# A new written-out order for the middle pairs, and five unread products behind the experts, in a fused attention, soft-mixture and gated kernel

## The chip, the cores and the metric

The kernel runs on one core of one Trainium2 chip. The time is device microseconds (us) of one execution. Engines are called PE (TensorE; PEld are its weight loads), DVE (VectorE), ACT (ScalarE), POOL (GpSimd) and SP (the queue that issues most DMAs). PEclk is the clock granted to PE, as a share of full speed.

## What is computed

```python
def reference(q, k, v, phi, w1, w2, w_gate, w_val, w_out, rms_g):   # cut to the formulas
    q_pool = q.reshape(4, 8, 576, 2, 64).mean(axis=3)       # q, k, v: 4 batches, 8 heads, 1152 x 64
    s = q_pool @ k.T / 8
    p = exp(s - s.max(-1));  a = (p / p.sum(-1)) @ v         # 576 x 64 a head
    x = a, heads side by side                               # 2304 tokens x 512
    logits = x @ phi                                        # 32 slots
    d = softmax of logits over all tokens;  slots = d.T @ x
    slot_out[e] = relu(slots[e] @ w1[e]) @ w2[e]            # 8 experts, 4 slots each
    x = softmax of logits over the slots @ slot_out
    xn = x / sqrt(mean(x * x) + 1e-6) * rms_g
    return (silu(xn @ w_gate) * (xn @ w_val)) @ w_out       # 1536 wide, result 2304 x 512
```

## The kernel before

**Stages.** Sixteen *pairs* of heads (p = 0 to 15) go through the attention one after the other, then come the eight experts, a short stage that multiplies small matrices out of the slots' outputs (lines 1110 to 1126), and the gated stage, whose product with w_out fills the end.

**The order of a pair is written out by hand.** Every engine takes its instructions in program order. For each pair a string of step names (FIRST for pair 0, PLAN for pairs 1 to 13, LAST_2 for pair 14, LAST for pair 15; lines 34 to 62) gives that order, and the loop at lines 853 to 871 calls one function a name. The steps that matter here, in pair p:

- `m` (wide_item, lines 311 to 335): a product of PE for the row maxima of pair p+1 into two PSUM banks, and a reduction of DVE over it. There are nine in a pair; the last three stand together behind `q81`.
- `q` and two digits (qk, line 374): eight products of PE into two PSUM banks: three parts of the scores, and a product (operands mr and pick) that subtracts the row maxima. Then an exponential on ACT (line 385). Eighteen in a pair.
- `e` and two digits (add_e, line 390): adds these tiles up on POOL (line 401; two operands in SBUF), for the sums of the rows. Fourteen of the eighteen issue an addition.
- `v` and a digit (av, line 403): 16 matmul records of PE, exponentials by values.
- `rest_k` (line 286) and `sum_q` (line 248): a DMA that adds into SBUF, issued on POOL's queue.
- `load_64`, `abs_64`, `turn_64`, `spill` (lines 639 to 704, 631): the three large matrices of the gated stage arrive as 64-bit numbers. `load_64` fetches 512 KB, `abs_64` makes two passes of ACT over it, `turn_64` one pass of DVE with two operands in SBUF (line 698), and `spill` writes the result to DRAM. There are up to three of each in a pair, 36 turned tiles in all.
- `load_ew` (line 776): a piece of the experts' weights.
- `sums`, `inverse`, `recips`, `x_turn`, `x_divide`, `x_logits`, `logit_add` (lines 418 to 502): what is left of pair p-1: its row sums, their inverses, the division and the logits.
- `high_q`, `low_q`, `round_k`, `less_k`, `block_q`, `max_red`, `max_row`, `send_row`, `ta`, `tb`: the operands of pairs p+1 and p+2, in two parts each, and the row of negated maxima, which four small DMAs of SP bring into the tile mr. `low_q` is a DVE pass with two operands in SBUF too (line 268).

**Buffers.** The two-bank PSUM tiles rotate through four buffers (line 176), so a product waits until the one four tiles earlier is read. SBUF tiles come from sets of equal slots (A, B, C, W). While pairs run, the tile of `v` (from `v0` to the next pair's `take_x`) holds one of the four PSUM buffers.

**hold** (line 198) issues products of constant tiles into a PSUM bank that nobody reads. Before the change it is used at lines 910, 926, 957 and 962, between the attention and the experts.

```python
PLAN = """
m take_x load_q q00 load_k sum_q q01 q10 m q11 q20 q21 e00 e10 e20 e01 m q30 q31 e30 e11 c_exp rest_k q40 m e21 e31
q41 e40 load_ew e41 q50 q51 m turn_64 q60 load_ew q61 e50 e60 q70 m q71 q80 q81 c_soft round_k abs_64 m round_k m m v0
...
```

Of the kernel before, what the change touches and what calls it, by code (L numbers as in the profile page):

```python
# [37 lines left out]
less_k ta v21 v41 v51 send_row v11 v71 v61 v81  # L38
"""
PLAN = """  # L40
m take_x load_q q00 load_k sum_q q01 q10 m q11 q20 q21 e00 e10 e20 e01 m q30 q31 e30 e11 c_exp rest_k q40 m e21 e31
q41 e40 load_ew e41 q50 q51 m turn_64 q60 load_ew q61 e50 e60 q70 m q71 q80 q81 c_soft round_k abs_64 m round_k m m v0
spill e51 v1 e61 sums e70 e80 e71 e81 max_red x_logits inverse inverse max_row load_v d_back v2 less_k v3 c_soft
abs_64 v4 high_q abs_64 v5 c_soft low_q block_q logit_add pair_up recips x_turn d_copy turn_64 slot_part x_divide
x_divide v6 d_turn tb d_exp slot_copy ta drop_x c_turn turn_64 load_64 slot_turn v7 load_64 send_row c_soft v8 load_64
"""
LAST_2 = """
m take_x load_q q00 load_k sum_q q01 load q10 m q11 load q20 load q21 e00 e10 e20 e01 m load q30 q31 e30 e11 c_exp
rest_k load q40 m e21 e31 load q41 e40 load_ew e41 load q50 q51 m turn_64 load q60 load_ew load q61 e50 e60 q70 m q71
load q80 q81 c_soft round_k abs_64 m round_k m m v0 spill e51 v1 e61 sums e70 e80 e71 e81 max_red x_logits inverse  # L50
inverse max_row load_v d_back v2 less_k v3 c_soft abs_64 v4 high_q abs_64 v5 c_soft low_q block_q logit_add pair_up
recips x_turn d_copy turn_64 slot_part x_divide x_divide v6 d_turn tb d_exp slot_copy ta drop_x c_turn turn_64 load_64
slot_turn v7 load_64 send_row c_soft v8 load_64
"""
LAST = """
take_x q00 load_64 sum_up sum_up load_q load_k load q01 e00 e01 c_exp turn_64 load_ew load q10 load q11 spill e10 e11
# [39 lines left out]
def attention_softmoe_gated_kernel(ctx: ExitStack, tc: tile.TileContext, kT, qT, vv, ip, cst, w1, w2, wg, wv, wo, rg, out):  # L96
# [15 lines left out]
    def take(tag, shape, dt, name):  # L112
        assert free[tag] > 0, (tag, name)
        free[tag] -= 1
        return pool.tile(shape, dt, tag=tag, bufs=size[tag], name=name)
# [4 lines left out]
    def B(shape, dt, name):  # L120
        return take("B", shape, dt, name)
# [53 lines left out]
    def two_banks(name):  # L175
        return ps.tile([128, 2, 512], F32, tag="u", bufs=4, name=name)

    def bank(shape, name):
        if not attention[0]:
            return ps.tile(shape, F32, tag="u", bufs=6, name=name)  # L180
        n = 1
        for x in shape[1:]:
            n *= x
        t = two_banks(name)[0:shape[0], 0, 0:n]
        if len(shape) == 3:
            t = t.rearrange("p (a b) -> p a b", a=shape[1])
        elif len(shape) == 4:
            t = t.rearrange("p (a b c) -> p a b c", a=shape[1], b=shape[2])
        return t
# [8 lines left out]
    def hold(o, n):  # L198

        for _ in range(n):  # L200
            pe.matmul(o, lhsT=pick[0], rhs=mr[1][:, 0:512], start=True, stop=True)
# [16 lines left out]
    tb = one.tile([128, 128], F32R, name="tb")  # L218
# [570 lines left out]
    with tc.manual_schedule():  # L789
# [317 lines left out]
        pull()  # L1107


        sos = B([128, 512], F32, "sos")  # L1110
        ac.copy(sos[:, 0:256], so[:, 0:256])
        dv.tensor_copy(sos[:, 256:512], so[:, 256:512])
        o = bank([128, 4, 32], "gto")
        for k in range(4):
            pe.matmul(o[:, k, :], lhsT=sos[:, 128 * k:128 * k + 128], rhs=stack[:, 0:32], start=True, stop=True)
        gT, soT = pt[:, 0], pt[:, 1]
        ac.copy(soT, o)
        dv.tensor_tensor(out=gT, in0=o, in1=rgt[:, :, None].to_broadcast([128, 4, 32]), op=ALU.mult)
        o = bank([128, 32], "gram")
        for k in range(4):  # L1120
            for i in range(4):
                pe.matmul(o[32 * i:32 * i + 32, :], lhsT=soT[:, k, :], rhs=soT[:, k, :], start=(k == 0), stop=(k == 3))
        gram = tb[:, 0:32]
        ac.copy(gram, o)
        dv.tensor_tensor(out=gram[64:128], in0=o[64:128], in1=f(gram[64:128]), op=ALU.subtract)
# [188 lines left out]
```

## Time and profile before

| what | value |
|---|---|
| three runs | 698.14, 704.37, 704.47 us; median 704.37 |
| the profiled execution | 706.88 us, its span 705.0 us |
| mean granted clock of PE | 0.983 |
| busy, share of the span | PE 95%, PEld 69%, POOL 64%, DVE 62%, ACT 57% |
| attention, pairs 0 to 15 | to 446 us |
| experts | about 459 to 498 us |
| gated stage | to the end |

The span runs from the first to the last instruction; 1.9 us of the execution lie around it. A busy share is an average over stages with different limits, so waits are read stage by stage below.

### The profile page before, as it was taken

To read this page: it belongs to the slowest core of one execution; us is meant where nothing else is said; L and a number is where in the kernel's file an instruction comes from. 1 tells how busy PE (TensorE), PEld (TensorE's weight loads), DVE (VectorE), ACT (ScalarE), POOL (GpSimd) and SP (SyncE) were. 2 spreads that over 40 slices of the span, in tenths; PEclk is the share of its full clock that TensorE was granted. 3 is DMA by queue.
4 is the path that set the end of the run, shared out by engine and by line. 5 is a ranking of instruction groups with operands and counts; after the bars stand their busy time and mean duration, and the time that the engine had idled before them with its cause. 6 is when DMAs were issued, how large, how long until landed. Compare 5 with 4: busy or idle time off the path is not lost.

```text
span 705.0 us, 17788 instructions
## 1 busy us (share of the span) xinstructions
PE 672.0 (95%) x7314; PEld 488.6 (69%) x7314; DVE 439.2 (62%) x595; ACT 400.8 (57%) x814; POOL 451.4 (64%) x368
## 2 busy tenths in 40 slices
PE   4999999999999999999999999999899999999998
PEld 3776775775766766757757666644577788888887
DVE  5766777777778788778788676421245755544420
ACT  3674974876768768647867544532146655444420
POOL 6689987978779779678797594000057855534420
PEclk9999999999999999999999999999689999999999
DMA  6345555966867765557466359899950100000000
GB/s 216 102 153 136 136 145 177 278 184 193 222 184 217 213 190 160 141 178 218 134 206 175 125 187 376 268 354 385 385 191 1 45 31 16 30 31 30 31 31 30
DMA packets 58040, 114.66 MB, mean 163 GB/s; under 512 B 6252, under 2 KB 20072, under 8 KB 57960
## 3 DMA queue, kind: packets, MB, share of 16 engines
q1 hardware_dynamic: 53928, 100.86, 41.2%
q0 software_dynamic: 4032, 12.68, 10.7%
q8 instruction: 57, 0.93, 0.5%
q14 instruction: 23, 0.19, 0.1%
HBM read 99.29 MB, written 14.16 MB: 161 GB/s over the span
## 4 chain that ended last, share of the span: by engine, by line
PE 85%; DVE 9%; DMA 2%; ACT 1%; POOL 1%; issue 1%; DVEq 0%; ACTq 0%; POOLq 0%
PE av L408 21%; PE yo L1215 20%; PE sc L383 17%; PE mxp L321 4%; DVE w L698 4%; DVE mx L322 4%; PE gv L1167 3%; PE sums L431 2%; PE hin L980 2%; PE xo L471 1%; PE so L1005 1%; PE part L1146 1%; DMA w<-in_w_dram 1%; PE mxp L331 1%; PE sumt L441 1%; PE xl L489 1%
## 5 line engine op out<-in xcount | busy, mean ns | idle before, releaser
L401 POOL TENSOR_TENSOR acc<-acc,e 128x576 f32<-128x576 f32 x153 | 230.0, 1516 | 10.9 <-ACT e L385 3.4
L385 ACT ACTIVATE e<-sc 128x576 f32<-128x576 f32 x288 | 167.8, 651 | 24.8 <-PE sc L383 19.4
L322 DVE TENSOR_REDUCE mx<-mxp 128x2 f32<-128x1024 f32 x120 | 145.4, 1224 | 57.4 <-PE mxp L321 57.4
L408 PE MATMUL av<-e,vt 128*32 128x288 f32 x2304 | 156.7, 415 | 0.0
L401 POOL TENSOR_TENSOR acc<-e 128x576 f32<-128x576 f32 x63 | 95.0, 1508 | 44.0 <-ACT e L385 44.0
L408 PEld LDWEIGHTS av<-e,vt 128*32 128x32 f32 x2304 | 69.2, 111 | 61.9 <-issue 9.7
L1215 PE MATMUL yo<-woh,hA 128*128 128x512 f32 (+1 forms) x312 | 98.7, 385 | 0.3 <-POOL hA L1198 0.2
L383 PE MATMUL sc<-qh,kh 64*128 64x288 f32 x576 | 87.9, 298 | 0.4 <-DVE mx L303 0.4
L383 PE MATMUL sc<-mr,pick 64*128 64x288 f32 x576 | 86.4, 293 | 0.0
L383 PE MATMUL sc<-qh,kl 64*128 64x288 f32 x576 | 86.4, 293 | 0.0
L383 PE MATMUL sc<-ql,kh 64*128 64x288 f32 x576 | 86.4, 292 | 0.0
L1198 POOL TENSOR_TENSOR hA<-hu,hA 128x384 fp32r<-128x384 f32 x48 | 48.8, 1018 | 43.6 <-ACT hA L1197 43.5
L1172 DVE SCALAR_TENSOR_TENSOR th<-th,gv 128x384 f32<-128x384 f32 x72 | 39.8, 553 | 57.3 <-ACT th L1169 57.1
L1215 PEld LDWEIGHTS yo<-woh,hA 128*128 128x128 f32 x312 | 57.6, 188 | 10.9 <-POOL hA L1198 1.1
L321 PE MATMUL mxp<-kh,qh 64*128 64x512 f32 x240 | 48.5, 420 | 16.6 <-DVE mx L322 16.6
L1169 ACT ACTIVATE th<-gv 128x384 f32<-128x384 f32 x72 | 35.2, 490 | 50.7 <-PE gv L1167 48.4
L383 PEld LDWEIGHTS sc<-qh,kl 64*128 64x128 f32 x576 | 55.6, 186 | 3.6
L383 PEld LDWEIGHTS sc<-qh,kh 64*128 64x128 f32 x576 | 55.3, 186 | 3.9 <-issue 0.9
L1215 PE MATMUL yo<-wol,hA 128*128 128x512 f32 (+1 forms) x151 | 57.8, 383 | 0.0
L383 PEld LDWEIGHTS sc<-mr,pick 64*128 64x128 f32 x576 | 55.7, 186 | 0.0
L383 PEld LDWEIGHTS sc<-ql,kh 64*128 64x128 f32 x576 | 55.5, 185 | 0.0
L698 DVE SCALAR_TENSOR_TENSOR w<-w,raw 128x512 uint32<-128x512 uint32 x36 | 51.9, 1443 | 0.0
(211 smaller groups left out, 1033.9 us busy)
## 6 DMA issues: line engine op xcount, KB each, us to landing
w<-in_w_dram SPq DMA_DIRECT2D x84, 256.0 KB
w<-in_w_dram SPq DMA_DIRECT2D x22, 512.0 KB
vt<-in_vv_dram SPq DMA_DIRECT2D x16, 576.0 KB
away<-w SPq DMA_DIRECT2D x36, 256.0 KB
w<-away SPq DMA_DIRECT2D x36, 256.0 KB
kraw<-in_kT_dram SPq DMA_DIRECT2D x15, 576.0 KB
kl<-in_kT_dram POOLq DMA_DIRECT2D x15, 576.0 KB, 5.8
raw<-in_wg_dram SPq DMA_DIRECT2D x12, 512.0 KB
```

The lines of the kernel that those rows point to most:

```text
L321: pe.matmul(o[:, s, :], lhsT=q[r, 128 * t:128 * t + 128], rhs=k[r, 512 * c:512 * c + 512], start=True, stop=True)
L322: dv.reduce_max(out=heads[:, :, t, c], in_=o, axis=AX.X)
L383: pe.matmul(o[:, s, 0:HQ], lhsT=w[r, wk], rhs=q[r, c], start=(i == 0), stop=(i == 3))
L385: ac.activation(ets[p, kt, h], o[:, :, 0:HQ], AF.Exp, scale=0.0625)
L401: eng.tensor_tensor(out=acc[p, h, j], in0=first[p, h, j] if n == 1 else acc[p, h, j], in1=e, op=ALU.add)
L408: pe.matmul(avt[p][g:g + 32, h, 0:HQ], lhsT=vt[p][:, kt, g:g + 32], rhs=ets[p, kt, h][:, g // 64], start=(n == 1), stop=(n == NKT))
L698: dv.scalar_tensor_tensor(out=y, in0=y, scalar=3, in1=lo, op0=ALU.logical_shift_left, op1=ALU.bitwise_or),
L1167: pe.matmul(o[i], lhsT=sg[n][:, 256 * i + 128 * c:256 * i + 128 * c + 128], rhs=cT[g], start=True, stop=True)
L1169: ac.activation(t, o[0], AF.Tanh, scale=0.5)
L1172: dv.scalar_tensor_tensor(out=t, in0=t, scalar=1.0, in1=o[0], op0=ALU.add, op1=ALU.mult)
L1198: gp.tensor_tensor(out=b, in0=u, in1=f(a), op=ALU.subtract)
L1215: pe.matmul(o, lhsT=x, rhs=w[:, c], start=(ft == 0 and i == 0), stop=(ft == NF - 1 and i == 2))
```

## The change

PLAN and LAST_2 get the same steps in another order; no step is added or taken away, and the `load` steps of LAST_2 keep their number. Behind the experts five unread products are issued, in three places.

```diff
 PLAN = """
-m take_x load_q q00 load_k sum_q q01 q10 m q11 q20 q21 e00 e10 e20 e01 m q30 q31 e30 e11 c_exp rest_k q40 m e21 e31
-q41 e40 load_ew e41 q50 q51 m turn_64 q60 load_ew q61 e50 e60 q70 m q71 q80 q81 c_soft round_k abs_64 m round_k m m v0
-spill e51 v1 e61 sums e70 e80 e71 e81 max_red x_logits inverse inverse max_row load_v d_back v2 less_k v3 c_soft
-abs_64 v4 high_q abs_64 v5 c_soft low_q block_q logit_add pair_up recips x_turn d_copy turn_64 slot_part x_divide
-x_divide v6 d_turn tb d_exp slot_copy ta drop_x c_turn turn_64 load_64 slot_turn v7 load_64 send_row c_soft v8 load_64
+take_x load_q m load_k sum_q q00 q01 q10 m q11 q20 e00 q21 m e01 e10 e20 e11 c_exp q30 e30 q31 rest_k q40 load_ew e21
+c_soft m e31 q41 e40 q50 e41 m e50 q51 q60 q61 q70 turn_64 m load_ew spill e60 q71 q80 q81 round_k round_k m m m e70
+e51 load_v e80 sums v0 v1 abs_64 e61 abs_64 e71 v2 d_back load_64 e81 max_red v3 v4 x_logits less_k inverse d_copy
+inverse high_q block_q c_soft max_row low_q x_turn recips abs_64 logit_add slot_part c_soft pair_up x_divide x_divide
+turn_64 v5 v6 d_turn send_row tb c_turn ta slot_copy turn_64 d_exp drop_x slot_turn c_soft v7 load_64 load_64 v8
 """
...
+        still = bank([128, 512], "hold")
+        hold(still, 2)
         sos = B([128, 512], F32, "sos")
         ac.copy(sos[:, 0:256], so[:, 0:256])
         dv.tensor_copy(sos[:, 256:512], so[:, 256:512])
         o = bank([128, 4, 32], "gto")
         for k in range(4):
             pe.matmul(o[:, k, :], lhsT=sos[:, 128 * k:128 * k + 128], rhs=stack[:, 0:32], start=True, stop=True)
+        hold(still, 1)
         gT, soT = pt[:, 0], pt[:, 1]
         ac.copy(soT, o)
...
                 pe.matmul(o[32 * i:32 * i + 32, :], lhsT=soT[:, k, :], rhs=soT[:, k, :], start=(k == 0), stop=(k == 3))
+        hold(still, 2)
         gram = tb[:, 0:32]
         ac.copy(gram, o)
```

LAST_2 is changed in the same way (its ten `load` steps stand between the score steps as before).

## Rows read from the trace of the kernel before

**Rows 1.** The page's 40 slices of the span: PE's granted clock in tenths.
```profile
PEclk9999999999999999999999999999689999999999
```

**Rows 2.** Waits of PE: waiter, releaser, us in total, times, longest.
```profile
PE mxp L321 <- DVE mx L322: 16.6, 11, 1.6
```

**Rows 3.** Timeline of PE in pairs 3 and 5: start, us, what, [idle before].
```profile
106.16 0.73 PE L321 MATMUL mxp<-kh,qh 64*128 64x512 f32 x4 [1.61 <-DVE mx L322]
...
156.43 0.40 PE L321 MATMUL mxp<-kh,qh 64*128 64x512 f32 x2
...
158.26 0.41 PE L321 MATMUL mxp<-kh,qh 64*128 64x512 f32 x2
...
161.79 0.73 PE L321 MATMUL mxp<-kh,qh 64*128 64x512 f32 x4 [1.55 <-DVE mx L322]
```

**Rows 4.** Timeline of DVE in pair 5.
```profile
156.87 1.23 DVE L322 TENSOR_REDUCE mx<-mxp 128x2 f32<-128x1024 f32 x1 [0.61 <-PE mxp L321]
158.01 2.59 DVE L698 SCALAR_TENSOR_TENSOR w<-w,raw 128x512 uint32<-128x512 uint32 x1
160.52 1.21 DVE L322 TENSOR_REDUCE mx<-mxp 128x2 f32<-128x1024 f32 x1
```

**Rows 5.** Timeline of POOL in pair 5.
```profile
156.34 1.44 POOL L401 TENSOR_TENSOR acc<-e 128x576 f32<-128x576 f32 x1
157.72 0.87 POOL L287 DMA_DIRECT2D kl<-in_kT_dram  x1
158.33 6.29 POOL L401 TENSOR_TENSOR acc<-acc,e 128x576 f32<-128x576 f32 x4
```

**Rows 6.** Line 698 by itself: min, median, max of its duration in ns.
```profile
L698 DVE SCALAR_TENSOR_TENSOR w<-w,raw x36: 669/1056/2656, 87.9 to 418.9; 128x512 uint32<-128x512 uint32 x36
```

**Rows 7.** Timelines of POOL and DVE: a pass in a lone issue, one among additions.
```profile
176.15 0.88 POOL L250 DMA_DIRECT2D qs<-in_qT_dram  x1 [2.18 <-PE pto L568]
...
176.54 0.68 DVE L698 SCALAR_TENSOR_TENSOR w<-w,raw 128x512 uint32<-128x512 uint32 x1
...
226.15 1.05 DVE L698 SCALAR_TENSOR_TENSOR w<-w,raw 128x512 uint32<-128x512 uint32 x1
```

**Rows 8.** Windows by pair (3, 7, 10): us, busy PE, PEld, DVE, ACT, POOL; clock.
```profile
93.51:121.94 28.43, 26.82 (x351) 18.74 (x351) 21.19 (x23) 18.80 (x35) 22.91 (x18) 0.94 0.60 168
...
205.19:231.88 26.69, 25.34 (x351) 18.20 (x351) 21.28 (x24) 20.39 (x43) 22.52 (x16) 1.00 0.75 218
...
288.02:316.88 28.86, 27.31 (x357) 19.42 (x357) 21.61 (x24) 18.78 (x35) 21.89 (x16) 0.94 0.55 164
```

**Rows 9.** Windows behind the experts, columns as in rows 8.
```profile
500.00:502.00 2.00, 1.49 (x44) 1.30 (x48) 0.53 (x3) 0.19 (x1) 0.00 (x0) 0.52 1.08 387
...
516.00:518.00 2.00, 2.00 (x15) 1.49 (x7) 0.77 (x2) 1.59 (x4) 1.50 (x3) 0.71 1.05 386
```

**Rows 10.** Timeline of PE behind the experts.
```profile
498.48 1.09 PE L1115 MATMUL gto<-cs,sos 128*128 128x32 f32 x8 [0.47 <-ACT sos L1111]
499.92 0.57 PE L1122 MATMUL gram<-pt 128*32 128x32 f32 x32 [0.35 <-ACT pt L1117]
501.00 0.82 PE L1035 MATMUL x<-tb,x2T 128*96 128x32 f32 x4 [0.51 <-DVE tb L1125]
501.75 1.94 PE L1146 MATMUL part<-w,pt 128*32 128x128 f32 x32
...
516.27 1.36 PE L1167 MATMUL gv<-cT,sg 128*128 128x384 f32 x4
...
520.77 1.08 PE L1146 MATMUL part<-w,pt 128*32 128x128 f32 x32
```

**Rows 11.** Timeline of PE: unread products at the attention's end.
```profile
450.88 1.89 PE L201 MATMUL hold<-mr,pick 128*128 128x512 f32 x7
```

**Rows 12.** Timelines of PE and SP in pair 7: four `v` steps, the last DMA of `send_row`.
```profile
222.59 4.09 PE L408 MATMUL av<-e,vt 128*32 128x288 f32 x64
...
224.89 0.55 SPq L357 DMA_DIRECT2D mr<-mrow  x1
```

More of the change, by code (lines that the diff above doesn't have):

```diff
@@ L46 @@
+c_soft m e31 q41 e40 q50 e41 m e50 q51 q60 q61 q70 turn_64 m load_ew spill e60 q71 q80 q81 round_k round_k m m m e70
+e51 load_v e80 sums v0 v1 abs_64 e61 abs_64 e71 v2 d_back load_64 e81 max_red v3 v4 x_logits less_k inverse d_copy
+inverse high_q block_q c_soft max_row low_q x_turn recips abs_64 logit_add slot_part c_soft pair_up x_divide x_divide
+turn_64 v5 v6 d_turn send_row tb c_turn ta slot_copy turn_64 d_exp drop_x slot_turn c_soft v7 load_64 load_64 v8
 """
 LAST_2 = """
-m take_x load_q q00 load_k sum_q q01 load q10 m q11 load q20 load q21 e00 e10 e20 e01 m load q30 q31 e30 e11 c_exp
@@ L49 @@
[L49 to L53, printed above, removed]
+take_x load_q m load_k sum_q q00 q01 load q10 m q11 load q20 e00 load q21 m e01 e10 e20 e11 c_exp load q30 e30 q31
@@ new lines @@
+rest_k load q40 load_ew e21 c_soft m e31 load q41 e40 load q50 e41 m e50 q51 load q60 load q61 q70 turn_64 m load_ew
+spill e60 q71 load q80 q81 round_k round_k m m m e70 e51 load_v e80 sums v0 v1 abs_64 e61 abs_64 e71 v2 d_back load_64
+e81 max_red v3 v4 x_logits less_k inverse d_copy inverse high_q block_q c_soft max_row low_q x_turn recips abs_64
+logit_add slot_part c_soft pair_up x_divide x_divide turn_64 v5 v6 d_turn send_row tb c_turn ta slot_copy turn_64
+d_exp drop_x slot_turn c_soft v7 load_64 load_64 v8
```

## The prediction, made before the result was seen

> **What bounds the kernel now.** I read the slices first. PE's granted clock is full nearly everywhere, with one dip after slice 28, around 500 us [rows 1]. PE is busy for 95% of the span, so the question is not which engine is busiest but where PE stands still. The list of PE's waits answers that: one wait stands out, the product of `m` for DVE's reduction four tiles earlier, 16.6 us in 11 places [rows 2]. The timeline of PE puts them once into each of the pairs 3 to 13, always at the first of the three `m` behind `q81`, about 1.5 us each; two of the eleven are shown [rows 3]. Nothing else makes PE wait in these pairs, so what removes this wait shortens the kernel directly.
>
> Why is DVE late there? In pair 5, DVE reduces the fifth `m` until 158.1, and the pass of `turn_64` that follows takes 2.59 us instead of 0.67. So the sixth `m`, whose product began at 158.26, is reduced only from 160.52 [rows 3, 4]; its two banks are what the seventh `m` needs. The fifth `m` shows that a reduction can begin 0.44 us behind its product (156.43 and 156.87), so this one could have begun at 158.70. It came 1.8 us late.
>
> The reason for the 2.59 us is seen on POOL. An addition ends at about 157.75, the issue of `rest_k` runs from 157.72 to 158.59, and four additions of 1.42 each (median) follow, 6.29 us with a hole of some 0.6 in them [rows 5]. A pass that begins at 158.01, inside the issue, and waits for the rest of the issue (0.58) and for the addition behind it (1.42) ends 0.67 later at 160.68; it ended at 160.60. Each of the 11 pairs has one such pass, and they are the longest of the 36, up to 2.66; the shortest takes 0.67, the median 1.06 [rows 6]. The issue alone does no harm: a pass that began inside an issue with no addition behind it took 0.68. Among additions one took 1.05, that is, it waited for the running one only [rows 7].
>
> **The new order, part by part.** *The pass leaves the issue.* In the queue of DVE `turn_64` still follows the fifth `m`. But that `m` now stands two score steps behind the fourth, not three. Between two `m` PE needs 1.83 us (156.43 to 158.26) [rows 3]. The product of `m` itself takes about 0.24 of it, so a score step takes 0.53. The pass therefore begins at 157.48 in the times of pair 5, while the addition of 156.34 still runs, 0.24 us before the issue begins at 157.72 [rows 4, 5]. POOL has the same additions ahead of `rest_k` (e10, e20, then e11 and e30 exchanged), so the issue does not come earlier. I expect the pass to get its turn when that addition ends, at 157.75, and to end at 158.4. The sixth `m`, whose place has not moved against the score steps, is then reduced from 158.70 to 159.9. The seventh was wanted at 161.79 less 1.55, that is at 160.24, so it no longer waits. This is -16.6 us, all of the wait of rows 2. What is late next is the ninth reduction at about 4 us behind that point, and nobody waits for it before the transposition of the maxima.
>
> *The clock of two pairs.* Pairs 3 and 10 are 1.7 us longer than their likes, and their mean clock is 0.94 where pair 7 has 1.00 [rows 8]. 0.06 of 28.4 and of 28.9 us is 1.7 each, 3.4 together. Both drops lie behind the wait. Without it PE has no pause in the pair; I take -3.4. The bounds are 0 (the drop has another cause) and -3.4.
>
> *The rest of the order.* No step is added, so every move costs what its waits cost. `sums` moves ahead of `v0`: its additions were done in the pair before. `recips` comes behind five `v` steps of about 1.0 us each [rows 12] and four smaller steps, and the `inverse` that it needs follows the ninth reduction directly, so PE has over 4 us of other work for it. Two `abs_64` come earlier, so the third is the only one behind `recips`. `load_64` issues one DMA ahead of `send_row` on SP and two behind it; `load_q` of the next pair comes behind these two, so `sum_q`, the first instruction of POOL in a pair, can move later by up to 2 or 3 us. POOL is busy for 22.5 of 26.7 us in pair 7, DVE for 21.3 [rows 8]. In a pair of 25.3 us POOL keeps 2.8 us of slack and DVE, less the 1.7 of waiting in the pass, 5.7. These two hide the moves. If `sum_q` took the slack, the additions would run into the next pair, where only `sums`, 12 us in, wants them.
>
> At the end of a pair the last `turn_64` can now fall among additions that still run: 1.05 for 0.68 [rows 7], 0.37 in each of 11 pairs, 4.1 us if nothing hides it and 0 if the four PSUM buffers do. I take half, +2.0.
>
> Pair 14 has no wait of this kind, so the new LAST_2 is worth 0. The DMAs of the experts' weights begin with that pair and move up with it. The steps that admit `load_ew` and `load_64` find room as often as before by the counts of free slots (10 pieces of weights and 36 matrices up to pair 13), so I cost them at 0.
>
> *The unread products.* Behind the experts the clock falls at 500.1 and is back only in the window from 516 to 518 [rows 9]. Ahead of the fall PE waits three times for ACT or DVE: 0.47, 0.35 and 0.51 us [rows 10]. Five unread products fill exactly these three places. Seven of them took 1.89 us, 0.27 each [rows 11], so five need 1.35 of the 1.33 us of waiting. They cost 0 where the wait covers them, and 1.35 at full clock, or 2.7 at half, without that cover; I take 0. What they may save: from 501.00 to 516.27 PE works at half clock; a group of 32 products takes 1.94 there and 1.08 at full clock [rows 10]. At that ratio 15.3 us become 8.5, a saving of 6.8. The waits for ACT and DVE inside it do not shrink. I take off 0.9, about two of them, and get -5.9; the bounds are +2.7 and -6.8. The value is near the lower end because between the attention and the experts, where such products stand already, the clock stays full [rows 1, 11].
>
> **The sum**, against the profiled execution of 706.88 us (span 705.0 and 1.9 around it): 706.9 - 16.6 - 3.4 + 2.0 - 5.9 = 683.0. The median of the runs is 2.5 us below the profiled execution, and the lowest is 8.7 below. Differences of that size are what one or two drops of the clock cost here. As the sum holds none, I take nothing more off.
>
> **The rivals.**
>
> *The clock falls behind the experts all the same.* For it: the last products of the experts wait for their weights before the first unread product, and nothing fills that. Against: the three places behind it are filled. 683.0 + 5.9 = 689, with up to 2.7 more.
>
> *The pass waits for a whole addition.* For it: the row of pair 7 shows a pass held by a running addition. If `sum_q` shifts the additions so that one begins just ahead of the pass at 157.48, the pass ends at 157.48 + 1.42 + 0.67 = 159.57, the sixth reduction at 160.8, and the seventh `m` waits 0.6: eleven times 0.6 is 6.6, so 690. Against: with POOL's times as they are, the running addition ends 0.27 after the pass begins. The Trainium skill ("SBUF — State Buffer", "Who interferes with whom") states this as a rule: of a VectorE instruction with two SBUF inputs and a GpSimd instruction that reads SBUF, whoever starts first has the shared pair for the whole instruction. The rows of the additions agree; the passes of 2.59 and 2.66 us do not, since by that rule a pass that finds only an issue running would not have waited. There the measurement decides.
>
> *The pass moves but the wait stays.* No row shows a pass that begins in an addition with an issue right behind it. If POOL's issue and the addition after it go first here too, the pass ends at 158.59 + 1.42 + 0.67 = 160.68, as before. Then only the unread products count: 706.9 - 5.9 = 701.
>
> *Slower: the row of maxima comes too late.* In pair 7 the last DMA of `send_row` is issued until 225.4 and the pair ends at 231.9, so 6.4 us were left [rows 8, 12]. In the new order the transposition that makes the row stands behind three more `v` steps, about 1.0 us each [rows 12], and the next pair is not later. That leaves 3.4, and some 0.7 to the first product that reads the row. It decides from a landing time of 4.1 us; the trace bounds that of these small DMAs only by the 6.4 above. At 6.4 every pair from 3 on would wait 2.3 us, and the score product of the first `q` holds everything behind it: 683 + 12 x 2.3 = 711. Against: these DMAs are small, and the one `load_64` ahead of them on SP is issued several us earlier.
>
> **How the numbers follow.** Chances: the forecast 0.56, clock falls anyway 0.15, whole addition 0.10, wait stays 0.10, slower 0.06; 0.03 is left. A measurement of this kernel can tell about 1% from no change, that is 7 us: faster is below 697.3, slower above 711.4. Forecast, clock and whole addition are faster (0.81, and part of the rest), the wait that stays is the same. The forecast's own range is 677 to 687: 4 us down for an uncovered tail that costs nothing and waits that shrink too, with the median's offset, and up for the full 4.1. For 8 in 10 the range has to take in 689 and 690 with their own tails: 676 to 697.
>
> **What would show it.** Right: PE's waits no longer list `m` behind DVE with more than 2 us in all; line 698 has a maximum near 1.5 and none at 2.4 or more; pair 7 lasts about 25.3 and pairs 3 and 10 about 25.3 and 25.7, at clock 1.00; the clock is full from 498 less 20 us on. Wrong: passes of 2.4 us or more behind the fifth `m`; a wait of `q00` for a DMA of mr; a pair of 26.5 us or more; a clock of 0.5 behind the experts.

## The result, and the profile after

The changed kernel takes 681.38 us (median of 4 runs, 680.55 to 682.14), the kernel before 703.66 (698.14 to 704.47 in 4 runs). The ratio is 0.970 with an interval of 0.965 to 0.975. The forecast was 683.0, within 676 to 697. The profiled execution after took 682.14 us with a span of 680.4.

The slices of the changed kernel, PE's granted clock, answer [rows 1]:

```profile
PEclk9999999999999999999999999999999999999999
```

Its waits of PE (waiter, releaser, us in total, times, longest) answer [rows 2]. These are the largest; the product of `m`, line 321, is not among them, nor further down:

```profile
PE mxp L301 <- ACT kh L817: 6.5, 3, 5.7
PE mxt L367 <- DVE mxw L363: 3.0, 1, 3.0
```

Both lie in the first 20 us and were there before. Line 698 by itself (min/median/max in ns) answers [rows 6]:

```profile
L698 DVE SCALAR_TENSOR_TENSOR w<-w,raw x36: 672/1166/1931, 65.7 to 379.4; 128x512 uint32<-128x512 uint32 x36
```

No pass takes 2.4 us or more. The median is 0.1 above that of before, but a second profile of the same kernel (experiment 7) has 1.06 again, so this shift is not steady. The windows of pairs 3, 7 and 10 answer [rows 8], with the same columns (us, then busy time of PE, PEld, DVE, ACT and POOL, then clock, DMA share, GB/s):

```profile
94.20:119.20 25.00, 24.98 (x351) 18.75 (x353) 20.02 (x22) 19.07 (x35) 22.62 (x19) 1.00 0.69 191
197.94:223.12 25.18, 25.15 (x351) 18.24 (x353) 21.02 (x24) 20.58 (x44) 20.50 (x15) 1.00 0.77 222
276.10:301.80 25.70, 25.68 (x357) 19.34 (x359) 21.82 (x26) 19.00 (x36) 22.36 (x16) 1.00 0.60 174
```

PE is now busy for all but 0.02 to 0.03 us of these pairs, so there is nothing left to take out of its waits here.

By stages, from the starts of `take_x` on ACT, the last product of the experts (`so`) and the first with w_out (`yo`), in us:

| stage | before | after | difference | forecast |
|---|---|---|---|---|
| up to pair 3 | 93.5 | 94.2 | +0.7 | 0 |
| pairs 3 to 13 | 306.1 | 286.4 | -19.8 | -16.6 - 3.4 + 2.0 = -18.0 |
| pairs 14 and 15, to the last `so` | 97.3 | 97.6 | +0.3 | 0 |
| last `so` to first `yo` | 21.0 | 15.1 | -5.9 | -5.9 |
| to the end | 187.1 | 187.1 | 0 | 0 |
| span | 705.0 | 680.4 | -24.6 | |

Of the 0.7 up to pair 3, 0.6 lies ahead of pair 1, where the two kernels are the same. The spans of the profiled executions differ by 24.6, the medians by 22.3. The other executions have no trace, but each has a mean granted clock of its own. Over all series of these experiments the kernel before ran at clocks from 0.983 to 1.00 and in 697.65 to 707.58 us; its two executions at 1.00 took 697.65 and 697.67. The changed kernel ran at 0.999 or 1.00 every time. At an undisturbed clock the two are thus about 16.5 us apart (697.7 and some 681), which is the wait of [rows 2]; the rest of the gain is clock, and differs from one execution of the kernel before to the next.

### The profile page after: what moved, and what is told of

Read it like the earlier page. It is cut to its first block, busy times and chain, and to the rows that moved or that the text cites. A ratio compares the mean times of both kernels' runs of the same rounds, so it can differ in the third digit from the quotient of the medians.

```text
span 680.4 us, 17782 instructions
## 1 busy us (share of the span) xinstructions
PE 663.7 (98%) x7319; PEld 487.2 (72%) x7319; DVE 432.7 (64%) x595; ACT 403.6 (59%) x814; POOL 457.4 (67%) x368
## 4 chain that ended last, share of the span: by engine, by line
PE 87%; DVE 4%; DMA 4%; issue 1%; ACT 1%; POOL 1%; DVEq 0%; POOLq 0%; ACTq 0%; SPq 0%
PE sc L383 22%; PE av L408 21%; PE yo L1219 19%; PE mxp L321 5%; PE gv L1171 3%; DMA w<-away 3%; PE sums L431 3%; PE hin L980 2%; PE xo L471 1%; DMA w<-in_w_dram 1%; PE so L1005 1%; PE mxp L331 1%; PE xl L489 1%; PE mxp L327 1%; PE pp L551 1%
## 5 line engine op out<-in xcount | busy, mean ns | idle before, releaser
L401 POOL TENSOR_TENSOR acc<-acc,e 128x576 f32<-128x576 f32 x153 | 233.3, 1541 | 9.9 <-ACT e L385 3.5
L408 PE MATMUL av<-e,vt 128*32 128x288 f32 x2304 | 151.0, 408 | 0.0
L408 PEld LDWEIGHTS av<-e,vt 128*32 128x32 f32 x2304 | 74.2, 110 | 61.1 <-issue 7.8
L401 POOL TENSOR_TENSOR acc<-e 128x576 f32<-128x576 f32 x63 | 100.8, 1601 | 17.1 <-ACT e L385 17.0
L698 DVE SCALAR_TENSOR_TENSOR w<-w,raw 128x512 uint32<-128x512 uint32 x36 | 44.9, 1248 | 0.3 <-ACT raw L696 0.3
```

The lines of the kernel that those rows point to most:

```text
L401: eng.tensor_tensor(out=acc[p, h, j], in0=first[p, h, j] if n == 1 else acc[p, h, j], in1=e, op=ALU.add)
L408: pe.matmul(avt[p][g:g + 32, h, 0:HQ], lhsT=vt[p][:, kt, g:g + 32], rhs=ets[p, kt, h][:, g // 64], start=(n == 1), stop=(n == NKT))
L698: dv.scalar_tensor_tensor(out=y, in0=y, scalar=3, in1=lo, op0=ALU.logical_shift_left, op1=ALU.bitwise_or),
```

## The experiments

Seven kernels take the change apart, and a small program measures the collision by itself. A ratio is always against the kernel before, run in the same series.

**1. The five products alone** (`hold_only`): the old order, with the three edits behind the experts.

```diff
+        hold(still, 2)
...
+        hold(still, 1)
...
+        hold(still, 2)
```

> The order of before, with the five unread products behind the experts alone. If they are what keeps the clock up there, the clock stays full from the end of the experts on and the time is 5.9 us below the kernel before (703.7 less 5.9: about 698), with the 16.6 us of waiting in the pairs untouched. Rival: the clock stayed up in the changed kernel because of the pairs (a denser attention), not of the products; then the clock falls here as before, and the time is that of before or up to 2.7 us more.

Measured: 699.36 us (696.46 to 702.02), ratio 0.996 (0.993 to 1.000). Its waits of PE:

```profile
PE mxp L321 <- DVE mx L322: 16.6, 11, 1.6
PE mxp L301 <- ACT kh L817: 5.8, 1, 5.8
```

The wait is unchanged to the tenth, so the products have no part in its going. From the last `so` to the first `yo` this profile has 15.1 us, as the changed kernel has. What the median gains is less, 4.2. The mean clock of its ten executions still goes from 0.994 to 1.00: the drops at the waits of `m` are left, and they come in some executions and not in others. Nor has every execution of the kernel before the whole fall behind the experts: 17 us at half clock take 0.012 off the mean, and six of the 13 in this series ran at 0.993 or more. In this profile pair 10 has the drop again (a mean clock of 0.94 from 286.19 to 315.04). Pair 3 has the same wait as before, but here the clock stayed full and the pair took 26.76 us, not 28.43 (compare [rows 8]):

```profile
93.50:120.26 26.76, 25.16 (x351) 18.16 (x351) 21.41 (x23) 18.75 (x35) 22.85 (x18) 1.00 0.64 178
```

**2. The order alone** (`order_only`): the new PLAN and LAST_2, without the products.

```diff
-        hold(still, 2)
...
-        hold(still, 1)
...
-        hold(still, 2)
```

> The new order without the five unread products. If the two parts are independent, the time is the changed kernel's 681.4 plus 5.8: about 687, with a clock of 0.5 for some 16 us behind the experts and no wait of m for DVE in the pairs. Rival: the products do nothing; then 681 to 682 and a full clock.

Measured: 683.68 us (682.89 to 685.88), ratio 0.973 (0.968 to 0.978). PE has no wait for `m`. The windows behind the experts in its profiled execution (us, PE busy, clock, DMA share, GB/s) show the fall and the return of the clock:

```profile
478.00:479.00 1.00, 0.71 (x7) 0.95 1.08 389
479.00:480.00 1.00, 0.65 (x32) 0.50 1.02 373
...
495.00:496.00 1.00, 1.00 (x14) 0.52 0.98 332
496.00:497.00 1.00, 1.00 (x7) 1.00 1.03 379
```

This execution took 685.88 at a mean clock of 0.987. The three others took 682.89 to 683.87 at 0.995, a smaller loss of clock. The expected time went by the full fall, and so came out too high: the fall is not the same in every execution.

**3. One product one step sooner** (`m_earlier`): of the whole new order only this, in PLAN and LAST_2, without the unread products.

```diff
-... e41 q50 q51 m turn_64 q60 ...
+... e41 q50 m q51 turn_64 q60 ...
```

> The order of before, but the fifth m one score step earlier (q50 m q51 turn_64), in PLAN and LAST_2: no instruction of POOL, ACT or SP moves. Theory A, the pass must begin ahead of the issue of rest_k: in pair 5 it begins at 8.46 us into the pair, 0.24 before the issue, takes 0.7 to 1.1, and the wait of m for DVE is gone: 16.6 us from that, 3.4 from the clock, so 684 beside 703.7. Theory B, the changed kernel gained because its additions and its issue came later (sum_q landed 2 to 5 us into the pair), and 0.24 us of lead is not enough: the pass still takes 2.5 or more, ends where it did, and the time stays within 3 us of before. Theory C, the pass is long for another reason than the issue and half a step of slack is simply half a step: the pass keeps 2.6 us, the wait falls from 1.5 to 1.0 a pair, and the time by about 6 us.

Measured: 684.33 us (682.66 to 686.60), ratio 0.974 (0.969 to 0.979). The wait is gone from PE's list in all 11 pairs. Line 698 by itself:

```profile
L698 DVE SCALAR_TENSOR_TENSOR w<-w,raw x36: 669/842/1556, 88.4 to 400.4; 128x512 uint32<-128x512 uint32 x36
```

The longest pass falls from 2.66 to 1.56. DVE's and POOL's steps keep their order; only the moment at which the pass begins is another. In pair 5, on POOL and then DVE:

```profile
153.87 0.85 POOL L287 DMA_DIRECT2D kl<-in_kT_dram  x1
```

```profile
153.66 0.82 DVE L698 SCALAR_TENSOR_TENSOR w<-w,raw 128x512 uint32<-128x512 uint32 x1
```

The pass begins 0.21 us ahead of the issue and takes 0.82; in the 11 pairs it begins 0.06 to 0.30 ahead and takes 0.68 to 0.92. So beginning in the issue costs the wait, and beginning ahead of it does not. It also means that most of the new order is not needed for its largest effect.

**4. The issue one place sooner** (`issue_earlier`): the other side of the collision. PE, DVE and ACT keep their orders.

```diff
-... q30 q31 e30 e11 c_exp rest_k q40 ...
+... q30 q31 e30 rest_k e11 c_exp q40 ...
```

> The order of before, but rest_k one addition earlier on POOL (ahead of e11), in PLAN and LAST_2: nothing moves on PE, DVE or ACT, and the pass of turn_64 begins where it did. Theory A: the issue of pair 5 runs from about 156.3 to 157.2, the addition of e11 from 157.2 to 158.6, the pass begins at 158.0 within that addition, waits for its end and takes 1.2 to 1.3; the sixth reduction begins at 159.3, and the seventh m waits 0.3 instead of 1.55: 11 times 1.2 is 13 us less, and 3.4 from the clock if its drops go too: 687 to 691 beside 703.7. Theory C, the issue is not the cause: passes of 2.6 and the time of before, 703 to 705.

Measured: 685.07 us (682.79 to 687.79), ratio 0.975 (0.969 to 0.980). Its wait for `m`, and line 698:

```profile
PE mxp L321 <- DVE mx L322: 1.1, 6, 0.2
...
L698 DVE SCALAR_TENSOR_TENSOR w<-w,raw x36: 670/1058/1556, 88.4 to 400.8; 128x512 uint32<-128x512 uint32 x36
```

The 1.56 is a later pass of a pair. In pair 5, on POOL and then DVE, the pass behind the fifth `m` is this:

```profile
152.27 0.86 POOL L287 DMA_DIRECT2D kl<-in_kT_dram  x1
152.87 1.72 POOL L401 TENSOR_TENSOR acc<-e 128x576 f32<-128x576 f32 x1
```

```profile
153.98 1.17 DVE L698 SCALAR_TENSOR_TENSOR w<-w,raw 128x512 uint32<-128x512 uint32 x1
```

It now comes behind the issue, in the addition that follows, and waits for the rest of that: in the 11 pairs it takes 1.02 to 1.27 us. What reaches PE is 0.1 to 0.2 in six pairs, less than the 0.3 a pair that I had put down, and most of the 16.6 is gone. So it is not where `m` stands that counts, but how the pass lies against the issue.

**5. The changed kernel, its fifth `m` a score step later** (`m_back`): a test of whether the one score step (0.53 us) that [rows 3 to 5] led me to is what saves the wait in the changed kernel.

```diff
-... q41 e40 q50 e41 m e50 q51 q60 ...
+... q41 e40 q50 e41 e50 q51 m q60 ...
```

> The changed kernel, but its fifth m back behind q51, one score step later, in PLAN and LAST_2; the rest of the new order and the unread products stay. In the changed kernel the pass begins 0.5 to 4.0 us ahead of the issue of rest_k in ten of the eleven pairs, because sum_q lands 2 to 5 us into the pair and the additions come later. Theory B (the later additions free the pass by themselves): begun 0.53 later it still misses the issue in nine or more pairs, no more than two pairs wait 1.5 us, and the time is 681 to 685. Theory A in its narrow form (the half step is what does it here too): the wait comes back in most pairs, 695 to 700.

Measured: 682.28 us (681.24 to 685.22), ratio 0.973 (0.969 to 0.979). Its profiled execution, the slowest of the four, has the wait in six places, 5.2 us in all. Pairs 6 and 13 have it longest, 1.61 and 1.27, and last 28.7 us each where the changed kernel has 25.5 and 27.5; the rest of pair 6's extra time is clock, which falls behind the wait (mean 0.94 from 172.50 to 201.16). Pair 6 on POOL, then on DVE and PE:

```profile
181.11 0.86 POOL L287 DMA_DIRECT2D kl<-in_kT_dram  x1
181.72 6.27 POOL L401 TENSOR_TENSOR acc<-acc,e 128x576 f32<-128x576 f32 x4
...
181.36 2.64 DVE L698 SCALAR_TENSOR_TENSOR w<-w,raw 128x512 uint32<-128x512 uint32 x1
183.92 1.21 DVE L322 TENSOR_REDUCE mx<-mxp 128x2 f32<-128x1024 f32 x1
...
185.19 0.73 PE L321 MATMUL mxp<-kh,qh 64*128 64x512 f32 x4 [1.61 <-DVE mx L322]
```

It is the old picture: the pass begins 0.25 into the issue, takes 2.64, and PE waits 1.61. But in the new order only two pairs have it, even with `m` where it was (in pair 13 the pass begins 0.56 into the issue). In the others the issue itself comes later. The four smaller waits, 0.29 to 0.92 in pairs 3, 4, 5 and 7, have another cause: passes of 1.34 to 1.96 that begin among additions, ahead of the issue. Pair 4 on POOL, then on DVE and PE:

```profile
127.20 1.43 POOL L401 TENSOR_TENSOR acc<-e 128x576 f32<-128x576 f32 x1
...
127.22 1.96 DVE L698 SCALAR_TENSOR_TENSOR w<-w,raw 128x512 uint32<-128x512 uint32 x1
...
130.37 0.73 PE L321 MATMUL mxp<-kh,qh 64*128 64x512 f32 x4 [0.92 <-DVE mx L322]
```

Here the addition begins 0.02 us ahead of the pass, which waits for all of it.

**6 and 7. The one swap with the products** (`m_earlier_hold`: experiment 3 with the edits of experiment 1), **beside the changed kernel once more** (`after_again`).

> The order of before with only the fifth m one score step earlier, and the five unread products. If the swap is the whole worth of the new order, this is as fast as the changed kernel: 681.4 within 1.5, no wait of m for DVE, full clock. If the rest of the new order is worth something (or costs something), the two differ by more than 1.5 us in the same series of runs.

> The changed kernel once more, beside the kernel above on the same chip: 680.5 to 682.5.

Measured: 682.73 us (681.59 to 683.23), ratio 0.973 (0.969 to 0.976), for the swap with the products, and 681.14 us (680.07 to 681.75), ratio 0.971 (0.967 to 0.974), for the changed kernel. All twelve executions have a clock of 0.999 or 1.00. The swap of one name thus brings all but 1.6 us of what the whole new order brings. The spans of the two profiled executions differ by 2.1: 0.5 of it lies ahead of pair 1, where the two kernels are the same, 0.6 in pairs 1 and 2 and 0.9 in pairs 3 to 13 (286.6 and 285.7). Which move is worth the 1.6 is open, and the two intervals overlap.

**8. The collision by itself** (`probe`). DVE makes a reduction of stepped length and then a pass of line 698's kind. Beside it POOL makes an addition, then (a) an issue with two additions behind it, (b) an issue alone, or (c) no issue and three additions. So the pass begins at stepped distances from the issue.

> A small program, not the kernel: it computes nothing of the reference and writes zeros. 37 trials. In each, a copy of ACT releases DVE and POOL together; DVE runs a reduction of one operand, longer by some 0.09 us from trial to trial, and then the pass of line 698 (two operands in SBUF); POOL runs an addition and then, in 18 trials, the issue of an accumulating DMA with two additions behind it, in 8 trials the issue alone, in 9 trials three more additions and no issue. x is the time from the begin of the issue to the begin of the pass. Theory A: for x below 0 the pass waits for the running addition (0.67 less x, up to 2.1); from some x between 0.06 and 0.24 to 0.87 it waits for the rest of the issue and a whole addition, 0.87 less x, and 1.42, and 0.67, so 2.1 to 2.9; with the issue alone it takes 0.67 to 0.7 at every x above 0; among additions 0.67 to 2.1. Rival: the issue holds the pass only until its own end, and then the pass goes first: 0.67 to 1.5 at every x above 0, and the 2.6 of the kernel have another cause.

Measured, in 35 trials: 18 of (a), 8 of (b), 9 of (c), with the first of (a), at the program's start, 3 us apart and left out below. Three trials of (a), each the issue on POOL and then the pass on DVE:

```profile
34.90 0.87 POOL L47 DMA_DIRECT2D kl<-in_kT_dram  x1
...
40.80 0.87 POOL L47 DMA_DIRECT2D kl<-in_kT_dram  x1
41.41 3.51 POOL L51 TENSOR_TENSOR acc<-acc,ee 128x576 f32<-128x576 f32 x2
...
115.65 0.87 POOL L47 DMA_DIRECT2D kl<-in_kT_dram  x1
```

```profile
35.02 0.68 DVE L44 SCALAR_TENSOR_TENSOR y<-y,raw 128x512 uint32<-128x512 uint32 x1
...
41.01 2.66 DVE L44 SCALAR_TENSOR_TENSOR y<-y,raw 128x512 uint32<-128x512 uint32 x1
...
116.91 1.60 DVE L44 SCALAR_TENSOR_TENSOR y<-y,raw 128x512 uint32<-128x512 uint32 x1
```

One trial of (b), the issue alone and the pass 0.48 into it:

```profile
139.46 0.87 POOL L47 DMA_DIRECT2D kl<-in_kT_dram  x1
...
139.94 0.68 DVE L44 SCALAR_TENSOR_TENSOR y<-y,raw 128x512 uint32<-128x512 uint32 x1
```

| pass begins after the issue's begin by | it takes | it ends after the issue's begin by |
|---|---|---|
| -0.15 to 0.12 (4 trials) | 0.68 to 0.75 | 0.60 to 0.80 |
| 0.21 | 2.66 | 2.87 |
| 0.55 | 2.30 | 2.85 |
| 0.90 | 1.95 | 2.85 |
| 1.26 | 1.60 | 2.86 |
| -0.02 to 0.73, issue alone (7 trials) | 0.68 | 0.66 to 1.41 |

The trials in between lie on the same line, and the eighth lone issue has a pass 0.13 ahead of it that takes 0.73. With an addition queued behind it, an issue shuts the pass out from somewhere between 0.12 and 0.21 us after its begin until a fixed point. The same issue with nothing behind it never does. So it is not the issue that holds the pass but the addition behind it, although by its record that begins only 0.6 us into the issue. The kernels agree: 0.29 into the issue, the pass of pair 5 before ended 2.88 after the issue's begin [rows 4, 5], and the one of pair 6 in experiment 5 ended 2.89 after it.

## Why the prediction was right

**The pass leaves the issue: -16.6. Right, and the cause is shown from both sides.** Moving the pass (experiment 3) removes the wait, moving the issue (experiment 4) removes all but 1.1 us of it, bringing them together again brings it back in the two pairs of experiment 5 where they meet, and the products leave it alone (experiment 1). The picture that I had drawn, a pass 0.2 us ahead of the issue, is the one of experiment 3, and it is enough by itself. What I had not seen is that the new order makes more room than that. I took POOL's times as they were, with the pass 0.24 us ahead of the issue. But `sum_q` comes 2.0 to 5.3 us into these pairs, where it came 1.5 us into one at the latest. I had noted that it could come later and had put that down to slack. Its data are asked for later, as forecast: for pair 3 `load_q` is issued at 92.28, 1.9 us ahead of the pair, where it was issued 4 us ahead before. The additions and `rest_k` move back with `sum_q`. In pair 3 of the changed kernel, on POOL and then DVE:

```profile
99.47 0.88 POOL L250 DMA_DIRECT2D qs<-in_qT_dram  x1 [1.89 <-ACT e L385]
...
103.31 1.89 POOL L401 TENSOR_TENSOR acc<-e 128x576 f32<-128x576 f32 x1
...
106.52 0.88 POOL L287 DMA_DIRECT2D kl<-in_kT_dram  x1
```

```profile
102.54 1.36 DVE L698 SCALAR_TENSOR_TENSOR w<-w,raw 128x512 uint32<-128x512 uint32 x1
104.03 1.23 DVE L322 TENSOR_REDUCE mx<-mxp 128x2 f32<-128x1024 f32 x1
```

The exponential of ACT that the row of `sum_q` names is no operand of it: the step adds into qs, which `load_q` fills. The issue comes 12.3 us into the pair (94.20), and the pass 4.0 ahead of it, among additions. In ten of the 11 pairs the pass begins 0.5 to 4.0 us ahead of the issue. In pair 13 it begins inside, at 0.06:

```profile
361.66 0.87 POOL L287 DMA_DIRECT2D kl<-in_kT_dram  x1
362.26 1.73 POOL L401 TENSOR_TENSOR acc<-acc,e 128x576 f32<-128x576 f32 x1
...
361.72 0.68 DVE L698 SCALAR_TENSOR_TENSOR w<-w,raw 128x512 uint32<-128x512 uint32 x1
```

It takes 0.68, as the probe's does at 0.03 and 0.12. By the probe 0.15 us more would have shut it out, and experiment 5, where the pass of that pair begins 0.56 into the issue, has the wait. So in the new order the later additions free the pass from the issue in most pairs. That one score step is worth 5.2 us in the profiled execution of experiment 5: it keeps the pass out of the issue in two pairs, and in four others it gives DVE room for a pass that additions hold up.

**The clock of pairs 3 and 10: -3.4. Right in this pair of executions.** They went from 28.4 and 28.9 to 25.0 and 25.7 at clock 1.00; 25.3 and 25.7 had been forecast, and pair 7 is at 25.2 for 25.3. But the drop is not tied to these pairs: experiment 1 has the wait in pair 3 at full clock, and the drop in pair 10 alone; experiment 5 has it in pair 6. In the traces the clock falls inside a pair only behind such a wait (in pair 3 before the wait ends at 106.16 and the fall comes at 107.6): behind four of the 24 waits that are longer than 1.2 us, and in none of the six traces that have no such wait. Where it falls belongs to the execution, and a median holds less of it. The forecast of 683.0 does not hang on this, since its sum takes the drops out of the execution that had them; that its change of 23.9 also comes near the 22.3 between the medians is partly luck.

**The last `turn_64` of a pair: +2.0. This is the term that was off; it measured 0.** The last passes did become longer, as I feared: in pairs 3 to 13 they take 11.4 us in all where they took 7.5, 3.9 more, near the 4.1 of the upper bound. But the 11 pairs lost 19.8 us, and the wait with the two clock drops makes 20.0, so next to nothing of it reached PE: it does not wait for any of these passes, which I put down to the four PSUM buffers. The lower bound was the value to take. The moves that I had costed at 0, `recips`, `sums` and `sum_q` among them, cost nothing in the pairs either, as far as the sum of the pairs can tell.

**The unread products: -5.9. Right in size, but it is not won in every execution.** The products fill the holes (timeline of PE after, where [rows 10] had waits of 0.47, 0.35 and 0.51), and groups of 32 products take 1.08:

```profile
479.14 0.73 PE L201 MATMUL hold<-mr,pick 128*128 128x512 f32 x2
479.71 1.06 PE L1117 MATMUL gto<-cs,sos 128*128 128x32 f32 x8
480.61 0.47 PE L201 MATMUL hold<-mr,pick 128*128 128x512 f32 x1
481.13 0.46 PE L1125 MATMUL gram<-pt 128*32 128x32 f32 x32
481.52 0.73 PE L201 MATMUL hold<-mr,pick 128*128 128x512 f32 x2
482.13 0.51 PE L1035 MATMUL x<-tb,x2T 128*96 128x32 f32 x4
482.57 1.08 PE L1150 MATMUL part<-w,pt 128*32 128x128 f32 x32
```

In `m_earlier` the same holes stand open, and its profiled execution kept the full clock through them:

```profile
480.81 1.09 PE L1115 MATMUL gto<-cs,sos 128*128 128x32 f32 x8 [0.47 <-ACT sos L1111]
482.25 0.46 PE L1122 MATMUL gram<-pt 128*32 128x32 f32 x32 [0.35 <-ACT pt L1117]
483.26 0.51 PE L1035 MATMUL x<-tb,x2T 128*96 128x32 f32 x4 [0.54 <-DVE tb L1125]
483.70 1.08 PE L1146 MATMUL part<-w,pt 128*32 128x128 f32 x32
```

From the last `so` to the first `yo` it has 15.1, as the changed kernel has, so the five products cost nothing. Holes of this size let the clock fall, but need not. One reading of the prediction was wrong: of the three waits of [rows 10] only two lie ahead of the fall at 500.1. The third lasts from 500.49 to 501.00, at half clock already, and in experiment 2 too the fall, at 478.9, comes ahead of it. Whether the two products in that place are needed, no run shows. The three kernels without the products in which the long waits of `m` are gone (experiments 2 to 4) ran 12 times: 8 times at a mean clock of 0.987 to 0.995, 4 times at 0.999 or 1.00. Only one of the 8 has a trace, that of experiment 2, so where the others lost their clock is inferred. The four kernels or series with the new or the swapped order and the products ran 20 times, always at 0.998 or more. So the products do what they were counted for; that an execution without them falls is likely, not certain. The new order with the products stands at a ratio of 0.971 (experiment 7), without them at 0.973: some 2 us of the median.

**The rivals.** *The clock falls all the same* did not happen in any execution with the products. *The pass waits for a whole addition* did happen, up to 1.93 us in all for the pass, but in the changed kernel the sixth `m` had room and PE waited for none. Its price, 0.6 a pair, was not paid there; in experiment 5, with `m` a score step later, passes that additions held up cost PE 0.29 to 0.92 in four pairs. *The wait stays* fell: an issue with additions behind it lets the pass go first that began earlier. *The row of maxima comes too late* fell: no score product waits for a DMA of mr in any trace of the new order.

The rule that the forecast weighed, in the Trainium skill ("SBUF — State Buffer", "Who interferes with whom"), that whoever begins first keeps the shared pair for its whole instruction, agrees with the probe's lone issues (0.68) and with its passes among additions (up to 1.86). It does not cover a pass that begins 0.4 us ahead of an addition's record and still waits for all of it; there the table of experiment 8 decides.

## What to carry to other kernels

Where a pass of VectorE over two SBUF operands takes several times its least duration, look in the timeline for what GpSimd has queued behind a DMA issue at the moment when the pass begins: a step moved by one place on either engine can be worth 16 us over 11 pairs. Test such a reading by moving each side of the collision alone, before the whole order is rewritten. And where PE has holes at half a microsecond each, read the mean clock of several executions before the profiled one is believed: a fall seen in one need not be in the next. With unread products in the holes behind the experts none of 20 executions here had it.

## What was not expected of the hardware

An addition queued behind an issue shuts the pass out ahead of its own record: from 0.12 to 0.21 us into an issue of 0.87, where the record of the addition begins at 0.6. In the trials with additions alone a pass that began 0.09 us ahead of an addition's record still took 0.68, so this head start belongs to the issue. And the same waits, 1.6 us in pair 3 or 0.3 to 0.5 us at a time behind the experts, come ahead of a fall of the clock to half in some executions and of none in others; what decides that, no run here shows.
